# Block-sparse attention, cosine router and experts on one core: routing steps tied behind their unit in the queues of VectorE and ScalarE

## The chip, the core and the metric

One core of a Trainium2 chip: TensorE (matmuls), VectorE, ScalarE, GpSimd and the SP queue, which issues most transfers. The names in the profile are PE, PEld (TensorE's weight loads), DVE (VectorE), ACT (ScalarE), POOL (GpSimd) and SP. Each engine works through its own queue in the order in which it was written at build time; where an instruction waits, everything behind it on that engine waits too. The metric is the device time of one execution in microseconds (us); lower is better.

## What is computed

Block-sparse attention on q, k, v of 4 sequences, 8 heads, 768 tokens, 64 columns, and on its output, 3072 rows of 512, a router that sends each row to the best of 8 experts:

```python
scores = (1 / sqrt(64)) * q @ k.T
scores = where(mask, scores, -1e9)        # window, first and last block, 3 random blocks of 32
attn   = softmax(scores) @ v              # (4, 8, 768, 64)
x      = attn.transpose(0, 2, 1, 3).reshape(3072, 512)

xn     = x / (norm(x) + 1e-6)
logits = xn @ en.T / tau                  # en: 8 normalised expert vectors
expert = argmax(logits);  gate = softmax(logits)[expert]
out[rows of e] = gate * (relu(x @ w1[e]) @ w2[e])     # w1 512x1024, w2 1024x512
```

## The kernel before

**Attention.** Heads are taken in pairs; a pair has two halves of 384 queries, a half six blocks of 128 keys. One block of keys is a **unit**: 12 units a pair, 48 a sequence, 192 in all (`attention_fast`, L735). A unit's work: `score_fast` (L287) makes `sc` on TensorE, mask included, and ScalarE's exponential of it, `e` (L300); `attend_fast` (L304) adds `e` into `esum` on VectorE (L313 for the second block, L315 for the later ones; the first block has no sum) and multiplies `e` with v into `av` on TensorE (L318). Scores are made two units ahead. `av` has one PSUM buffer: after a half's last block ScalarE copies one part of it (`part`, L322) and VectorE adds the other to it, giving `at` (L324); only then may `av` of the next half begin. After the sixth block of each half `turn_fast` (L267) turns half of the next pair's keys and queries: matmuls into `turn`, then `kt` on VectorE (L283) and after it `qt` on ScalarE (L284).

**Settling a half.** Three units into the next half, `settle` (L328) turns `at` back on TensorE (`back`, L346 and L353; the router's products are computed along with it) and VectorE divides: `dens`, `inv`, `x`, `part` (L356 to L364). `squares` (L368) then sums the squares of x on GpSimd: one product and seven halving additions into `nsq`. `turn`, `back`, `rk`, `slot_ps` and the first expert tile's transposes share one PSUM buffer (`two_banks`).

**Routing.** When a sequence's 48 units are done, its rows are routed beside the next sequence's units. `route` (L418) is a generator in four steps: sums of squares (`nrm`, L427), GpSimd's power for the root (L428) and the logits' sum `l` (L436); normalising and the maximum (L438 to L443); the exponential `ex_l` on ScalarE (L446) and the choice of the expert, `oh` (L449 to L452); the gate (L455 to L457), x out to memory on the SP queue (L460), and on GpSimd the running counts `seen` (L464). `rank` (L468) counts rows by expert, three small matmuls `rk` and three VectorE steps. After sequence 1, `dispatch_early` (L561) gives the first two sequences' rows places in 5 expert tiles, in nine steps; `fetch` issues the first tiles' weights and rows, `prepare` turns the first tile's rows. The plan in `after_sequence` (L698) names the local unit (counted from 0 in each sequence) ahead of whose `attend_fast` each step is called.

**What sets the order.** The text's order is a proposal only: at build time a scheduler lists each engine's instructions by a model of when they become ready. It may put a step well ahead of the unit with which it is called.

**Experts.** 27 tiles of 128 rows, each 32 + 32 matmuls (`hp`, L676, two passes each), ReLU to `h` (L679 on ScalarE, L683 on VectorE), transposes of the next tile's rows, 8 matmuls `yp` (L689) and the gate's product (L691). Inside the first tile `last_rows` (L835) settles the last half, sums its squares and routes the last sequence; `between` (L826) ranks it and places the late rows.

Of the kernel before, what the change touches and what calls it, by code (L numbers as in the profile page):

```python
# [11 lines left out]
F32 = mybir.dt.float32  # L12
I32 = mybir.dt.int32
BF16 = mybir.dt.bfloat16
ACT = mybir.ActivationFunctionType
ALU = mybir.AluOpType
# [3 lines left out]
P = 128  # L20
B, H, S, D = 4, 8, 768, 64
# [265 lines left out]
def score_fast(k, u):  # L287

    nc = k.nc
    g, qh, kc = u // (2 * NC), u // NC % 2, u % NC  # L290
    kt, qt = [t.rearrange("p c r t -> p (c r t)") for t in k.turned[g]]
    ps = k.big.tile([P, 2, 512], F32, name="sc", tag="big")
    queries = slice(qh * HALF, (qh + 1) * HALF)
    quarters = [(h, r, slice(kc * P + D * r, kc * P + D * (r + 1))) for r in range(2) for h in range(2)]
    for rows, cols, first in ((k.kmask, k.qmask, True), (kt, qt, False)):
        for h, r, keys in quarters:
            nc.tensor.matmul(ps[D * r:D * (r + 1), h, 0:HALF], lhsT=rows[D * h:D * (h + 1), keys],  # L297
                             rhs=cols[D * h:D * (h + 1), queries], start=first, stop=not first)
    e = k.ep.tile([P, 2, HALF], F32, name="e", tag="e")
    nc.scalar.activation(e, ps[:, :, 0:HALF], ACT.Exp)  # L300
    k.es[u] = e


def attend_fast(k, u):  # L304
    nc = k.nc
    g, qh, kc = u // (2 * NC), u // NC % 2, u % NC
    e, v = k.es[u], k.loaded[g][2]
    if kc == 0:
        k.av = k.acc.tile([P, 2, 512], F32, name="av", tag="av")
        k.first = e  # L310
    elif kc == 1:
        k.esum = k.sp.tile([P, 2, HALF], F32, name="esum", tag="esum")
        nc.vector.tensor_tensor(out=k.esum, in0=k.first, in1=e, op=ALU.add)  # L313
    else:
        nc.vector.tensor_tensor(out=k.esum, in0=k.esum, in1=e, op=ALU.add)  # L315
    for r in range(2):
        for h in range(2):
            nc.tensor.matmul(k.av[D * h:D * (h + 1), r, 0:HALF], lhsT=v[D * r:D * (r + 1), h, kc, :],  # L318
                             rhs=e[D * r:D * (r + 1), h, :], start=(kc == 0), stop=(kc == NC - 1))
    if kc == NC - 1:  # L320
        part = k.sp.tile([P, HALF], F32, name="part", tag="part")
        nc.scalar.copy(out=part, in_=k.av[:, 1, 0:HALF])  # L322
        at = k.sp.tile([P, HALF], F32, name="at", tag="at")
        nc.vector.tensor_tensor(out=at, in0=k.av[:, 0, 0:HALF], in1=part, op=ALU.add)  # L324
        k.done[u // NC] = (at, k.esum)
# [42 lines left out]
def squares(k, w):  # L368

    nc = k.nc  # L370
    b, j, qh = w // (2 * NPAIR), w // 2 % NPAIR, w % 2
    chunks = slice(qh * NQ, (qh + 1) * NQ)
    x = k.x[b][:, chunks, j * P:(j + 1) * P]
    sq = k.sp.tile([P, NQ, P], F32, name="sq", tag="sq", bufs=1)
    nc.gpsimd.tensor_tensor(out=sq, in0=x, in1=x, op=ALU.mult)  # L375
    width = P // 2
    while width:
        out = sq[:, :, 0:width] if width > 1 else k.nsq[b][:, chunks, j:j + 1]
        nc.gpsimd.tensor_tensor(out=out, in0=sq[:, :, 0:width], in1=sq[:, :, width:2 * width], op=ALU.add)  # L379
        width //= 2  # L380


def count_good(k):
# [314 lines left out]
def after_sequence(n, b):  # L698

    routing = partial(next, route(n, b), None)  # L700
    plan = [(7, routing), (9, routing), (10, routing), (12, routing), (13, partial(rank, n, b))]
    if b == EARLY - 1:
        step = partial(next, dispatch_early(n), None)
        plan += [(u, step) for u in (15, 16, 18, 20, 21, 22, 23, 24, 25)]
        plan += [(27, partial(fetch, n, 0)), (28, partial(fetch, n, 1)), (43, partial(prepare, n, 0))]
    return plan


def attention_fast(n, ctx):
# [25 lines left out]
    for u in range(units):  # L735
        g = u // per
        if u % per == 0 and g + 2 < pairs:
            load_pair(n, g + 2)
        if u % NC == 3 and NC < u < units - 2 * NC:
            settle(n, u // NC - 1)  # L740
        if u % NC == 4 and NC < u < units - 2 * NC:
            squares(n, u // NC - 1)
        if u % (per * NPAIR) == 0 and u:
            plan = after_sequence(n, u // (per * NPAIR) - 1)
        for when, what in plan:
            if when == u % (per * NPAIR):
                what()
        attend_fast(n, u)
        if u + 2 < units:
            score_fast(n, u + 2)  # L750
        if u % NC == NC - 1 and g + 1 < pairs:
            turn_fast(n, g + 1, u % per // NC)
        if u in (units - NC - 1, units - 2):
            settle(n, u // NC - 1)
        if u == units - 4:
            squares(n, 2 * B * NPAIR - 3)


def attention_exact(n, ctx):
# [53 lines left out]
def fast(n):  # L813
    n.rings = {}
    with ExitStack() as ctx:
# [18 lines left out]

        def last_rows():  # L835
            settle(n, 2 * B * NPAIR - 1)
            squares(n, 2 * B * NPAIR - 2)
            squares(n, 2 * B * NPAIR - 1)
            for _ in route(n, B - 1):
                pass  # L840

# [90 lines left out]
```

## Time and profile before

| | |
|---|---|
| median of 3 runs | 807.51 us (807.42 to 809.67) |
| the profiled execution | 808.88 us |
| its span, first to last instruction | 807.2 us |
| TensorE busy | 754.6 us, 93% |
| VectorE, ScalarE, GpSimd busy | 41%, 25%, 25% |
| granted TensorE clock, mean | 0.98 |

The profiled execution's time lies 1.7 us above its span, which is what goes on around the first and the last instruction. TensorE is busy nearly throughout: attention fills the span up to about 397 us, the expert tiles the rest. Shares over the whole span say little of single stages; the rows below cut out the stretches in which a finished sequence is routed, and a quiet stretch beside them.

### The profile page before, as it was taken

The numbers are of one execution on the slowest core, as the hardware profiler recorded it, in microseconds if no ns is written. First come the engines' busy times: TensorE is split into PE (matmuls) and PEld (weight loads), VectorE is DVE, ScalarE is ACT, GpSimd is POOL, SyncE is SP. The second block draws the span as 40 slices with busy tenths as digits, with TensorE's granted clock in tenths as the row PEclk, the third lists the DMA queues.
The fourth block names the chain that finished last, engine by engine and source line by source line (L and its number), as shares of the span: only waits on it lengthen the run. The fifth ranks groups of instructions, "written<-read, shape, count | busy, mean of one in ns | idle before, by whom it ended". The sixth has DMA issues, their size and how long they took to land.

```text
span 807.2 us, 22564 instructions
## 1 busy us (share of the span) xinstructions
PE 754.6 (93%) x10028; PEld 492.9 (61%) x10028; DVE 327.1 (41%) x645; ACT 200.3 (25%) x292; POOL 205.2 (25%) x362
## 2 busy tenths in 40 slices
PE   5999979999698996999999999999999999999992
PEld 2555545555355553555676777867768677686770
DVE  3666665667576665566564111111111111111110
ACT  2555534555344453455300000000000000000000
POOL 2133342443325534234431211112111121110210
PEclk9999998999899998999999999999999999999997
DMA  4112215111349303200379998998999989889890
GB/s 157 25 59 62 62 60 218 55 45 45 138 154 401 129 31 126 74 2 4 122 278 406 332 341 323 321 339 299 338 323 322 343 309 335 329 317 334 302 327 15
DMA packets 64100, 165.48 MB, mean 205 GB/s; under 512 B 2988, under 2 KB 15276, under 8 KB 63222
## 3 DMA queue, kind: packets, MB, share of 16 engines
q1 hardware_dynamic: 59238, 149.60, 52.2%
q0 software_dynamic: 4480, 13.91, 4.4%
q8 instruction: 82, 1.34, 0.7%
q10 hardware_dynamic: 272, 0.39, 0.2%
q14 instruction: 28, 0.23, 0.1%
HBM read 148.14 MB, written 16.54 MB: 204 GB/s over the span
## 4 chain that ended last, share of the span: by engine, by line
PE 81%; issue 5%; DVE 5%; POOL 2%; ACT 2%; DMA 1%; another core or an unknown queue 0%; SPq 0%; POOLq 0%; DVEq 0%; ACTq 0%
PE hp L676 21%; PE yp L689 20%; PE sc L297 17%; PE av L318 15%; PE turn L280 2%; PE back L353 2%; ACT e L300 1%; PE xg_ps L661 1%; DVE esum L315 1%; PE back L346 1%; POOL sq L379 1%; DMA out_dram<-y,slot_l 1%; POOL nrm L428 1%; DMA emb<-in_moe_expert_emb_dram 1%; DVE esum L313 1%
## 5 line engine op out<-in xcount | busy, mean ns | idle before, releaser
L676 PEld LDWEIGHTS hp<-xgt,w 128*128 128x128 f32 x1728 | 197.1, 192 | 13.6 <-issue 11.5
L676 PE MATMUL hp<-xgt,w 128*128 128x128 f32 x1728 | 198.1, 275 | 1.4 <-DVE at L324 1.4
L689 PE MATMUL yp<-w,h 128*128 128x512 f32 x432 | 190.1, 592 | 0.9 <-DVE h L683 0.9
L300 ACT ACTIVATE e<-sc 128x768 f32<-128x768 f32 x192 | 155.4, 810 | 128.5 <-PE sc L297 124.5
L318 PE MATMUL av<-e,vld 64*64 64x384 f32 x1536 | 166.3, 500 | 20.0 <-DVE at L324 18.9
L315 DVE TENSOR_TENSOR esum<-esum,e 128x768 f32<-128x768 f32 x128 | 133.2, 1041 | 76.1 <-ACT e L300 73.8
L297 PE MATMUL sc<-qt,kt 64*64 64x384 f32 x1536 | 161.8, 489 | 0.1
L689 PEld LDWEIGHTS yp<-w,h 128*128 128x128 f32 x432 | 79.9, 190 | 91.7 <-issue 89.9
L679 ACT ACTIVATE h<-hp 128x512 f32<-128x512 f32 x27 | 16.1, 598 | 359.8 <-PE hp L676 359.8
L379 POOL TENSOR_TENSOR sq<-sq 128x192 f32<-128x192 f32 (+2 forms) x192 | 96.4, 502 | 15.1
L318 PEld LDWEIGHTS av<-e,vld 64*64 64x64 f32 x1536 | 51.4, 135 | 73.3 <-ACT e L300 24.2
L692 POOL DMA_INDIRECT out_dram<-y,slot_l x22 | 22.1, 1005 | 267.7 <-DVE y L691 255.6
L297 PEld LDWEIGHTS sc<-qt,kt 64*64 64x64 f32 x1536 | 60.1, 136 | 41.5 <-issue 38.9
L683 DVE TENSOR_SCALAR h<-hp 128x512 f32<-128x512 f32 x27 | 18.7, 692 | 160.1 <-PE hp L676 159.8
L375 POOL TENSOR_TENSOR sq<-x 128x384 f32<-128x384 f32 x32 | 26.9, 840 | 222.2 <-DVE part L364 168.3
L691 DVE TENSOR_SCALAR y<-yp,xg 128x512 f32<-128x512 f32 x27 | 20.3, 751 | 152.7 <-PE yp L689 152.7
L297 PE MATMUL sc<-qmask,kmask 64*64 64x384 bf16 x768 | 68.0, 330 | 0.0
L297 PEld LDWEIGHTS <-kmask 64*64 64x64 bf16 x768 | 25.2, 109 | 34.2 <-issue 34.1
L313 DVE TENSOR_TENSOR esum<-e 128x768 f32<-128x768 f32 x32 | 30.9, 966 | 16.8 <-ACT e L300 16.8
L284 ACT ACTIVATE qt<-turn 128x384 f32<-128x384 f32 x32 | 15.7, 491 | 49.5 <-DVE kt L283 49.5
L645 POOL DMA_INDIRECT xg<-x_dram,slot_l x24 | 24.8, 1032 | 7.4 <-issue 7.4
L353 PE MATMUL back<-ones,esum 64*64 64x1 f32 x1536 | 26.5, 191 | 0.0
(157 smaller groups left out, 374.6 us busy)
## 6 DMA issues: line engine op xcount, KB each, us to landing
w<-in_moe_w_dram SPq DMA_DIRECT2D x58, 2048.0 KB, 10.6
x_dram<-x SPq DMA_DIRECT2D x4, 1539.0 KB
kld<-in_k_dram SPq DMA_DIRECT2D x16, 384.0 KB, 4.5
vld<-in_v_dram SPq DMA_DIRECT2D x16, 384.0 KB, 3.3
qld<-in_q_dram SPq DMA_DIRECT2D x15, 384.0 KB, 5.6
x_early<-x SPq DMA_DIRECT2D x2, 1539.0 KB
qld<-in_q_dram ACTq DMA_DIRECT2D x1, 384.0 KB
xg<-x_dram,slot_l POOLq DMA_INDIRECT x24, 7.6
```

The source lines that it names most:

```text
L297: nc.tensor.matmul(ps[D * r:D * (r + 1), h, 0:HALF], lhsT=rows[D * h:D * (h + 1), keys], rhs=cols[D * h:D * (h + 1), queries], start=first ...
L300: nc.scalar.activation(e, ps[:, :, 0:HALF], ACT.Exp)
L313: nc.vector.tensor_tensor(out=k.esum, in0=k.first, in1=e, op=ALU.add)
L315: nc.vector.tensor_tensor(out=k.esum, in0=k.esum, in1=e, op=ALU.add)
L318: nc.tensor.matmul(k.av[D * h:D * (h + 1), r, 0:HALF], lhsT=v[D * r:D * (r + 1), h, kc, :], rhs=e[D * r:D * (r + 1), h, :], start=(kc == 0 ...
L353: nc.tensor.matmul(sums[D * s:D * (s + 1), t, h, r:r + 1], lhsT=esum[D * r:D * (r + 1), h, cols], rhs=k.ones[D * r:D * (r + 1), 0:1], star ...
L375: nc.gpsimd.tensor_tensor(out=sq, in0=x, in1=x, op=ALU.mult)
L379: nc.gpsimd.tensor_tensor(out=out, in0=sq[:, :, 0:width], in1=sq[:, :, width:2 * width], op=ALU.add)
L645: nc.gpsimd.indirect_dma_start(out=x[:, :], out_offset=None, in_=(k.x_dram if late else k.x_early)[:, :], in_offset=bass.IndirectOffsetOnA ...
L676: nc.tensor.matmul(hp[:, f, :], lhsT=w1[:, d, (f0 + f) * P:(f0 + f + 1) * P], rhs=xt[:, d, :], start=(d == 0), stop=(d == ND - 1))
L689: nc.tensor.matmul(yp, lhsT=h[:, f, :], rhs=w2[:, f, :], start=(f == 0), stop=(f == NF - 1))
L692: nc.gpsimd.indirect_dma_start(out=k.out[:, :], out_offset=bass.IndirectOffsetOnAxis(ap=slot, axis=0), in_=y[:, :], in_offset=None, bounds ...
```

## The change

Three edits. First, `score_fast` and `attend_fast` keep the last exponential and the last `esum` that they wrote, and every step of the plan is now called inside two blocks that tie each VectorE instruction of the step behind that `esum`, and each ScalarE instruction behind that exponential, in the engine's queue. It is an order only, no wait is added; instructions on other engines are not tied. Second, the plan calls nearly every step one unit later. Third, the squares of the last half go from GpSimd to ScalarE, one activation with an accumulator for each of three chunks, and the squares of the half before are called two units before the end of attention instead of in `last_rows`.

```diff
@@ score_fast
-    nc.scalar.activation(e, ps[:, :, 0:HALF], ACT.Exp)
+    k.exps = nc.scalar.activation(e, ps[:, :, 0:HALF], ACT.Exp)
@@ attend_fast (the same for the second block's sum, L313)
-        nc.vector.tensor_tensor(out=k.esum, in0=k.esum, in1=e, op=ALU.add)
+        k.summed = nc.vector.tensor_tensor(out=k.esum, in0=k.esum, in1=e, op=ALU.add)
@@ new
+def last_squares(k, w):
+    b, j, qh = w // (2 * NPAIR), w // 2 % NPAIR, w % 2
+    for c in range(qh * NQ, (qh + 1) * NQ):
+        sq = k.sp.tile([P, P], F32, name="sq_l", tag="sq_l")
+        k.nc.scalar.activation(sq, k.x[b][:, c, j * P:(j + 1) * P], ACT.Square,
+                               accum_out=k.nsq[b][:, c, j:j + 1])
@@ after_sequence
-    plan = [(7, routing), (9, routing), (10, routing), (12, routing), (13, partial(rank, n, b))]
+    plan = [(8, routing), (10, routing), (11, routing), (13, routing), (14, partial(rank, n, b))]
-        plan += [(u, step) for u in (15, 16, 18, 20, 21, 22, 23, 24, 25)]
-        plan += [(27, partial(fetch, n, 0)), (28, partial(fetch, n, 1)), (43, partial(prepare, n, 0))]
+        plan += [(u, step) for u in (16, 17, 18, 20, 21, 22, 23, 24, 26)]
+        plan += [(28, partial(fetch, n, 0)), (29, partial(fetch, n, 1)), (44, partial(prepare, n, 0))]
@@ attention_fast
-                what()
+                with n.tc.issue_after(n.summed.ins), n.tc.issue_after(n.exps.ins):
+                    what()
-        if u == units - 4:
-            squares(n, 2 * B * NPAIR - 3)
+        if u >= units - 4 and u % 2 == 0:
+            squares(n, 2 * B * NPAIR - 3 + (u == units - 2))
@@ last_rows
-            squares(n, 2 * B * NPAIR - 2)
-            squares(n, 2 * B * NPAIR - 1)
+            last_squares(n, 2 * B * NPAIR - 1)
```

What the scheduler makes of it, at three places. Line numbers of the changed kernel from L392 on are 9 higher than before (`nrm<-nsq` is L427 before and L436 after, `l<-part` L436 and L445).

VectorE, where sequence 0 is routed, before: from the end of the `settle` that gives the sequence's last x.

```order
L364 TENSOR_TENSOR part<-back,inv 128x3x16
L436 TENSOR_REDUCE l<-part 128x48
L427 TENSOR_REDUCE nrm<-nsq 128x6
L438 TENSOR_SCALAR nrm<-nrm 128x6
L439 RECIPROCAL nrm<-nrm 128x6
L441 TENSOR_TENSOR l<-l,nrm 128x48
L442 TENSOR_REDUCE mx<-l 128x6
L315 TENSOR_TENSOR esum<-esum,e 128x768
L443 TENSOR_TENSOR l<-l,mx 128x48
L449 TENSOR_SCALAR pick<-l 128x48
L450 TENSOR_TENSOR pick<-pick,rev 128x48
```

The same place after.

```order
L364 TENSOR_TENSOR part<-back,inv 128x3x16
L315 TENSOR_TENSOR esum<-esum,e 128x768
L324 TENSOR_TENSOR at<-av,part 128x384
L313 TENSOR_TENSOR esum<-e 128x768
L436 TENSOR_REDUCE nrm<-nsq 128x6
L283 COPY kt<-turn 128x2x3x64
L445 TENSOR_REDUCE l<-part 128x48
L315 TENSOR_TENSOR esum<-esum,e 128x768 x2
L447 TENSOR_SCALAR nrm<-nrm 128x6
L448 RECIPROCAL nrm<-nrm 128x6
L450 TENSOR_TENSOR l<-l,nrm 128x48
L451 TENSOR_REDUCE mx<-l 128x6
```

Before, `nrm<-nsq` and what needs it stand directly behind `part` and ahead of the half's last `esum` and of `at`; after, those two, the next half's first `esum` (L313) and more come first.

VectorE, where the early dispatch ends, before (`ge`, `val` and `lanes` are its tables of places).

```order
L585 SCALAR_TENSOR_TENSOR pos<-late,pos 128x12
L523 TENSOR_TENSOR ge<-pos,by_g 128x72
L526 TENSOR_REDUCE hi<-ge 128x12
L528 SCALAR_TENSOR_TENSOR low<-hi,pos 128x12
L529 TENSOR_TENSOR ge<-ge 128x12x5
L541 TENSOR_TENSOR lanes<-lane,low 128x384
L532 TENSOR_TENSOR val<-ge,tok_f 128x12x5 x2
L541 TENSOR_TENSOR lanes<-lane,low 128x384 x2
L315 TENSOR_TENSOR esum<-esum,e 128x768
L356 TENSOR_REDUCE dens<-back 128x6
L541 TENSOR_TENSOR lanes<-lane,low 128x384
L357 TENSOR_SCALAR dens<-dens 128x6
```

The same stage after: from `taken`, the rows that each expert takes, on.

```order
L587 SCALAR_TENSOR_TENSOR taken<-end_3772,base 128x8
L513 CAST expert_e<-ex 128x5
L315 TENSOR_TENSOR esum<-esum,e 128x768
L521 TENSOR_TENSOR at_e<-oh,base 128x96
L524 TENSOR_REDUCE pos<-at_e 128x12
L521 TENSOR_TENSOR at_e<-oh,taken 128x96
L593 TENSOR_TENSOR pos<-pos,rank 128x12
L524 TENSOR_REDUCE taken_t<-at_e 128x12
L592 TENSOR_TENSOR late<-rank,taken_t 128x12
L594 SCALAR_TENSOR_TENSOR pos<-late,pos 128x12
L324 TENSOR_TENSOR at<-av,part 128x384
```

Before, the tables of places stand ahead of the half's last sum and `at`; after, only the steps up to `pos` do, `ge` and all that follow it come behind L313.

ScalarE, from the last `part` of attention into the first expert tiles, before.

```order
L300 ACTIVATE e<-sc 128x768 x5
L322 COPY part<-av 128x384
L679 ACTIVATE h_6300<-hp_0_6301 128x512
L446 ACTIVATE ex_l<-l 128x48
L679 ACTIVATE h_6531<-hp_1_6532 128x512
```

After.

```order
L300 ACTIVATE e<-sc 128x768 x5
L322 COPY part<-av 128x384
L688 ACTIVATE h_6309<-hp_0_6310 128x512
L388 ACTIVATE sq_l,nsq<-x 128x128 x3
L455 ACTIVATE ex_l<-l 128x48
L688 ACTIVATE h_6528<-hp_1_6529 128x512
```

The three squares stand between the first tile's ReLU and the routing's exponential.

## Rows read from the trace of the kernel before

**Rows 1.** Busy time by stretch: length, five engines' busy time (instructions), PEclk, DMA, GB/s

```profile
110.95:130.37 19.42, 13.26 (x248) 7.00 (x242) 9.75 (x28) 5.76 (x9) 6.29 (x15) 0.82 0.40 164
130.37:142.61 12.24, 11.47 (x254) 6.70 (x246) 7.62 (x16) 5.62 (x8) 4.26 (x8) 1.00 0.34 99
142.61:153.34 10.73, 10.72 (x248) 6.11 (x242) 7.30 (x13) 5.62 (x8) 4.21 (x8) 1.00 0.01 3
226.19:251.55 25.36, 22.43 (x494) 12.90 (x486) 19.92 (x61) 11.24 (x16) 8.81 (x16) 1.00 0.63 221
251.55:276.09 24.54, 23.49 (x500) 13.75 (x493) 15.08 (x29) 11.24 (x16) 13.96 (x20) 1.00 0.68 259
309.63:328.69 19.06, 12.91 (x248) 6.89 (x243) 9.75 (x27) 5.76 (x9) 6.28 (x15) 0.82 0.21 84
```

**Rows 2.** Waits of TensorE, whole span: waiting, released by, total us, times, longest

```profile
PE av L318 <- DVE at L324: 18.9, 4, 6.2
PE rk L474 <- ACT qt L284: 2.3, 3, 0.8
PE turn L280 <- DVE part L364: 1.8, 1, 1.8
PE yp L689 <- DVE h L683: 0.9, 1, 0.9
PE first L661 <- ACT qt L284: 0.8, 1, 0.8
PE slot_ps L551 <- ACT qt L284: 0.7, 1, 0.7
```

**Rows 3.** Timeline of VectorE in the first route: start, us, instruction, idle before

```profile
115.89 0.18 DVE L427 TENSOR_REDUCE nrm<-nsq 128x6 f32<-128x24 f32 x1 [2.68 <-POOL nsq L379]
117.54 0.17 DVE L438 TENSOR_SCALAR nrm<-nrm 128x6 f32<-128x6 f32 x1 [1.47 <-POOL nrm L428]
118.33 0.95 DVE L315 TENSOR_TENSOR esum<-esum,e 128x768 f32<-128x768 f32 x1
120.78 0.56 DVE L324 TENSOR_TENSOR at<-av,part 128x384 f32<-128x384 f32 x1 [0.33 <-ACT part L322]
```

**Rows 4.** Timeline of VectorE in an undisturbed stretch

```profile
152.47 0.96 DVE L315 TENSOR_TENSOR esum<-esum,e 128x768 f32<-128x768 f32 x1 [0.65 <-ACT e L300]
156.75 0.56 DVE L324 TENSOR_TENSOR at<-av,part 128x384 f32<-128x384 f32 x1 [0.37 <-ACT part L322]
157.84 0.96 DVE L313 TENSOR_TENSOR esum<-e 128x768 f32<-128x768 f32 x1 [0.53 <-ACT e L300]
158.73 0.55 DVE L283 COPY kt<-turn 128x384 f32<-128x384 f32 x1
160.53 2.02 DVE L315 TENSOR_TENSOR esum<-esum,e 128x768 f32<-128x768 f32 x2 [1.26 <-ACT e L300]
```

**Rows 5.** Timeline of GpSimd: squares in the first route, then in the undisturbed stretch

```profile
113.25 2.33 POOL L379 TENSOR_TENSOR sq<-sq 128x192 f32<-128x192 f32 x6
...
155.65 3.51 POOL L379 TENSOR_TENSOR sq<-sq 128x192 f32<-128x192 f32 x6
159.24 0.20 POOL L379 TENSOR_TENSOR nsq<-sq 128x3 f32<-128x3 f32 x1
```

**Rows 6.** Timeline of TensorE in the undisturbed stretch

```profile
160.55 0.88 PE L318 MATMUL av<-e,vld 64*64 64x384 f32 x8
```

**Rows 7.** Timelines: ScalarE's only square, then GpSimd and VectorE in the first tile

```profile
7.78 0.63 ACT L166 ACTIVATE emb_sq<-emb 8x512 f32<-8x512 f32 x1 [5.24 <-DMA emb<-in_moe_expert_emb_dram]
8.32 0.19 ACT L166 ACTIVATION_READ_ACCUMULATOR emb_sq<-emb 8x1 f32 x1
...
403.57 0.83 POOL L375 TENSOR_TENSOR sq<-x 128x384 f32<-128x384 f32 x1 [3.49 <-DVE part L364]
...
407.22 0.18 DVE L427 TENSOR_REDUCE nrm<-nsq 128x6 f32<-128x24 f32 x1 [2.10 <-POOL nsq L379]
409.92 0.69 DVE L683 TENSOR_SCALAR h<-hp 128x512 f32<-128x512 f32 x1 [0.20 <-issue]
```

More of the change, by code (lines that the diff above doesn't have):

```diff
@@ L312, in attend_fast @@
         k.esum = k.sp.tile([P, 2, HALF], F32, name="esum", tag="esum")
-        nc.vector.tensor_tensor(out=k.esum, in0=k.first, in1=e, op=ALU.add)
+        k.summed = nc.vector.tensor_tensor(out=k.esum, in0=k.first, in1=e, op=ALU.add)
     else:
-        nc.vector.tensor_tensor(out=k.esum, in0=k.esum, in1=e, op=ALU.add)
+        k.summed = nc.vector.tensor_tensor(out=k.esum, in0=k.esum, in1=e, op=ALU.add)
     for r in range(2):
```

## Prediction

> **What bounds the kernel now.** I read the table of busy time by stretch first, cut at the starts of the `dens` step (L356), which comes once per half pair of heads. An undisturbed half pair lasts 10.73 us, and TensorE is busy for 10.72 of it, as in the stretch 142.61:153.34 [rows 1]: the attention half of the program runs at TensorE's pace, and whatever makes TensorE wait there lengthens the program one for one. From the first expert tile on, the list of waits names for TensorE only the 0.9 us at L689 [rows 2]; the rest is its own matmuls. So all that can be gained lies in waits of TensorE, and the same table shows where: the half pair in which a finished sequence is routed takes 19.42 us the first time and 19.06 the last; there are three such, after sequences 0, 1 and 2, and I take 19.2 for the middle one. Against 10.73 they lose 8.69, 8.5 and 8.33, together **25.5 us**. The half pair after each, with the ranking, takes 12.24: 1.51 too much.
>
> The list of waits says for what: `av` matmuls (L318) wait for VectorE's `at` (L324), 18.9 us in four waits, 6.2 the longest [rows 2]. VectorE's own timeline shows why `at` was late [rows 3]. In its queue `nrm` (L427) stood ahead of the running unit's `esum`; it waited 2.68 us for GpSimd's squares, then L438 waited 1.47 us for GpSimd's power, and only then came `esum`, the rest of the routing and `at`, at 120.78. [...]
>
> **The change part by part.**
>
> *Routing on VectorE (first edit and plan).* The order shows that the steps now stand where the text puts them: `nrm<-nsq` behind the `esum` of local unit 7, the next five steps behind that of unit 9, the one-hot steps inside the next `dens` chain, the gate's three ahead of `at`. So both waits for GpSimd leave the place ahead of `esum` and `at`. What is late next? I lay the new order over the undisturbed stretch.
> - First wait. There the squares' last add ended at 159.24 + 0.20 = 159.44 [rows 5] and `esum` L313 at 157.84 + 0.96 = 158.80 [rows 4]. So `nrm` still waits 0.64 us, runs 0.18, and `kt` (L283), due at 158.73, starts 0.9 us late. Queued behind `kt` are `qt` and the next exponential on ScalarE, and `av` on TensorE waits for that one: `esum` at 160.53 waited for it and `av` at 160.55 started with it [rows 4, 6], so there is no slack. I charge **0.9 us** of TensorE per route; bounds 0 (squares in time) and 2.7 (the wait of now [rows 3]).
> - What TensorE does not pay: the 0.9 us reduction `l<-part` falls into the gap of 1.26 before `esum` at 160.53 [rows 4]; the power, 1.5 us after `nrm`, runs beside two `esum`s of 2.02 us together, so L438 no longer waits.
> - Five short steps then stand before the next `esum`. Four took 117.54 to 118.33, 0.79 us [rows 3], five 1.0, against a gap of 0.65 [rows 4]: 0.35 late. Four more inside the `dens` chain fill its gaps, some 0.15; the gate's three, 0.55, stand against a gap of 0.37 before `at` [rows 4]. With 0.3 us given back at the `esum` between and TensorE a little behind `at`, **0.4 us** per route; bounds 0 and 0.9.
> - The clock: the waits that are left are of the size of the 1.8 us that TensorE waited at `turn` [rows 2], and the stretch with that one was granted 1.00, 226.19:251.55 [rows 1]. I charge nothing.
>
> So a route costs 1.3 instead of 8.5: 25.5 − 3 × 1.3 = **21.6 us** saved.
>
> What slows the squares shows in one row each: the six adds took 2.33 us while VectorE stood, and 3.51 beside its `esum`s [rows 5]. [...]
>
> *Ranking, one unit later.* TensorE's `rk` waited for `qt`, 2.3 us in three [rows 2], because it needs the PSUM buffer that `qt` was still reading. A unit later `qt` is over. Now GpSimd decides: its six `seen` adds stand alternating with the next squares, so the counts come about as late as TensorE does (their durations beside `esum`s are in no row). I charge 0.2 (0 to 0.8, the wait of now) instead of 0.77; the matmuls' own 0.75 (11.47 − 10.72 [rows 1]) stay. Saved: 3 × 0.57 = **1.7 us**. `count`, `mine` and `rank` now stand behind one more `esum`, ahead of which nothing on TensorE waits for them until `back`, a unit later.
>
> *Early dispatch (after sequence 1).* The two half pairs that hold ranking and dispatch take 25.36, 3.90 over 21.46; without the ranking's 1.51 the dispatch costs 2.4, seen as TensorE's 1.8 at `turn` and 0.4 at `at` [rows 1, 2]. VectorE was busy 19.92 instead of 14.60 there, so some 5.3 us of its work are the cause, and none of it goes away. By the place of the steps in the new order I estimate that 3.5 us of that stand ahead of `at` of unit 17 and 2.9 behind it, with the pauses between short dependent steps. The gaps there are 0.65, 0.3 and 0.37; with an estimated 0.5 that VectorE is ahead after `rk`, that leaves 1.7 late, and the rest against the next half pair's gaps 0.4. **2.1 instead of 2.4: 0.3 saved**; bounds 0 and 3.5 for the cost. `slot_ps` and the first tile's transposes move behind `qt` too: their waits of 0.7 and 0.8 [rows 2] go, **1.5 saved**. The rest of the stretch 251.55:276.09, some 2 us too long beside 8 MB of weights, stays as it is; the weights' and the rows' issues on the SP queue move by a unit and are needed only after the end of attention.
>
> On the SP queue the copies of `x` now stand between a pair's `vld` and `kld`, so `kld` waits for the gate's end, under 1 us later than now; the pair is turned one and a half pairs, some 30 us, later. Nothing.
>
> *Last squares on ScalarE.* Now GpSimd starts them at 403.57, `nrm` waits 2.10 us and runs at 407.22, L438 follows after the power, and `h` (L683) stands behind it at 409.92; TensorE waits 0.9 for `h` [rows 2, 7]. The order has three squares with an accumulator read each. The only such pair in the trace took 0.63 + 0.19 on 512 columns [rows 7], so at most 0.82 each on 128 columns, 2.5 us from 403.5: `nrm` runs before 406.1, at least 1.1 us earlier, and so does `h`, less 0.2 for L443 that now stands ahead of it. That covers the 0.9: **0.9 saved**, and as ScalarE's next work, the exponential, waits for the same chain, no cost. The squares of the half pair before only change their place in the text; GpSimd waits for their data as now.
>
> **The sum.** 21.6 + 1.7 + 0.3 + 1.5 + 0.9 = **26.0 us**. Against the profiled execution's own 808.88 us that gives 782.9. That execution lies 1.4 above the median of the runs, 807.51, so I predict **781.5**.
>
> **The rivals.**
> - *All hidden.* The waits that I charge (3 × 1.5 and 2.1, 6.6 us) vanish, as squares come in time and gaps take all steps: 774.9. For it speaks that several are under 1 us; against it that `av` at 160.55 has no slack.
> - *The wait moves and stays long.* `nrm` ahead of `kt` waits as it does now ahead of `esum`: 2.7 and the power's 1.5 come to stand before `kt`, the clock falls again for 2.3: 6.5 instead of 1.3 per route, 797.1. It decides if GpSimd ends its squares over 2 us later than in the undisturbed stretch. Against it: the overlay has them beside the same `esum`s already.
> - *No effect.* The order names a wait that was not the limit, and TensorE stands as long for another: 807.5. Against it, all three routes show the same rows.
> - *Slower: ScalarE is shut.* `ex_l` now stands behind the exponential of unit 12 and ahead of `part`, some 3 us after L443 should be through. Should L443 come more than 3 us late, exponentials and `part` queue behind `ex_l`, TensorE stands and its clock falls; from 12 us late on (3 + the 8.5 of now) each route is dearer than today. At 15 us, 3 × (12 + 2.5) = 43.5 against 25.5: 825. Nothing in rows 3 to 5 makes so long a chain.
>
> **How the numbers follow.** Forecast 0.75, all hidden 0.11, wait moved 0.09, no effect 0.02, slower 0.03. The forecast's own bounds: every charge at its lower end 774.9; step one at 2.7, the gate at 0.9, ranking at 0.8, dispatch at 3.5 make 5.4 + 1.5 + 1.8 + 1.4 = 10.1 more, 791.6. Both ends at once everywhere are unlikely; **776 to 789** leaves out about 2 in 10. A change under 0.3% (2.4 us) could not be told from none: faster 0.94, same 0.03, slower 0.03.
>
> **What would show it.** Right: no wait of `av` for `at` above 2 us after sequences 0 and 2; half pairs with routing of 11.5 to 12.5 us at a granted clock of 1.00; `nrm<-nsq` waiting under 1 us; `rk` not waiting for `qt`; `yp` not for `h`. Wrong: a stretch at half clock after a route, a long idle before `kt`, `ex_l` or `rk`, or `turn` waiting for a dispatch step for over 2 us.

## The result and the profile after

The changed kernel takes **781.9 us** (median of 4 executions, 780.66 to 785.54) against 807.46 for the kernel before in the same runs: ratio 0.9683 (95% interval 0.9652 to 0.9714), **25.6 us faster**. I had predicted 781.5, as 26.0 us. Two later sets of executions, on two chips, gave 780.51 at a ratio of 0.9672 (0.9659 to 0.9684) and 780.95 at 0.9668 (0.9651 to 0.9686).

The profiled execution of the first set took 785.54 (span 783.6), 3.6 us more than its median. Where it can't be read alone I set the profile of the second set beside it (span 779.9).

Busy time by stretch, changed kernel, cut at `dens` as [rows 1]: length, busy time of PE, PEld, DVE, ACT and POOL (with instructions), granted clock, DMA share, GB/s. First the three half pairs from the first route on, an undisturbed one, the first half pair of the second and third route, then the four half pairs of ranking, dispatch and weights after sequence 1 (49.90 us in the two stretches of [rows 1]), and the half pair with the last `at`:

```profile
111.56:123.41 11.85, 11.01 (x252) 6.21 (x246) 9.09 (x20) 5.51 (x8) 5.49 (x9) 1.00 0.01 2
123.41:135.11 11.70, 11.35 (x250) 6.82 (x246) 8.91 (x23) 5.74 (x9) 5.08 (x14) 1.00 0.65 198
135.11:146.88 11.77, 11.05 (x248) 7.05 (x243) 7.29 (x13) 5.61 (x8) 3.54 (x8) 1.00 0.44 176
146.88:157.62 10.74, 10.73 (x248) 6.13 (x243) 7.38 (x14) 5.61 (x8) 4.13 (x8) 1.00 0.37 113
200.54:212.40 11.86, 11.01 (x252) 6.23 (x247) 9.10 (x21) 5.51 (x8) 5.47 (x9) 1.00 0.01 3
295.00:306.85 11.85, 11.01 (x252) 6.22 (x246) 9.10 (x20) 5.51 (x8) 5.49 (x9) 1.00 0.01 3
212.40:262.30 49.90, 46.04 (x982) 29.08 (x978) 36.83 (x96) 22.70 (x33) 21.70 (x42) 1.00 0.87 302
372.79:381.39 8.60, 7.17 (x113) 6.58 (x106) 1.66 (x7) 1.07 (x2) 3.28 (x10) 0.80 0.83 283
```

The stretch with a route took 19.42 us at a clock of 0.82 and takes 11.85 at 1.00; all three show the same. In the trace of before the clock is 0.50 from 120.0 to 126.5 us, around the end of the 6.16 us that `av` waited for `at`. Two things are new: the third stretch, which took 10.73 before, takes 11.77, and the four half pairs of dispatch are as long as they were, though their waits for `qt` are gone. The list of TensorE's waits (us in total, times, longest) says what stands there now:

```profile
PE av L318 <- ACT e L300: 4.4, 5, 1.7
PE sc L297 <- issue: 2.3, 3, 1.1
PE hp L685 <- DVE at L324: 1.4, 1, 1.4
PE av L318 <- DVE at L324: 1.0, 3, 0.4
```

The 18.9 us that `av` waited for `at` [rows 2] have become 1.0; the waits at `rk`, `turn`, `yp`, `first` and `slot_ps` are no longer in the list. "issue" is a stop for which the profile has no releaser.

What remains of a route stands in the timeline of the first one, GpSimd, VectorE and TensorE (start, us, instruction, idle before it), to be read against [rows 3]:

```profile
113.86 3.50 POOL L379 TENSOR_TENSOR sq<-sq 128x192 f32<-128x192 f32 x6
117.67 0.18 DVE L436 TENSOR_REDUCE nrm<-nsq 128x6 f32<-128x24 f32 x1 [0.66 <-POOL nsq L379]
117.77 0.55 DVE L283 COPY kt<-turn 128x384 f32<-128x384 f32 x1
119.59 0.88 PE L318 MATMUL av<-e,vld 64*64 64x384 f32 x8 [0.84 <-ACT e L300]
...
127.18 0.52 DVE L324 TENSOR_TENSOR at<-av,part 128x384 f32<-128x384 f32 x1
127.75 0.88 PE L318 MATMUL av<-e,vld 64*64 64x384 f32 x8 [0.35 <-DVE at L324]
```

`nrm` still waits for GpSimd, 0.66 us now, with `kt` behind it, and `av` pays 0.84 for that; the gate ahead of `at` costs 0.35. Each value comes again in the other two routes.

In the tail the squares now take ScalarE 0.9 us, and `nrm` no longer waits:

```profile
382.69 0.31 ACT L388 ACTIVATE sq_l<-x 128x128 f32<-128x128 f32 x1 [1.91 <-DVE x L361]
382.91 0.19 ACT L388 ACTIVATION_READ_ACCUMULATOR sq_l<-x 128x1 f32 x1
383.49 0.19 ACT L388 ACTIVATION_READ_ACCUMULATOR sq_l<-x 128x1 f32 x1
383.89 0.17 DVE L436 TENSOR_REDUCE nrm<-nsq 128x6 f32<-128x24 f32 x1
386.82 0.69 DVE L692 TENSOR_SCALAR h<-hp 128x512 f32<-128x512 f32 x1 [0.20 <-DMA w<-in_moe_w_dram]
```

### The profile page after: what moved, and what is told of

It reads as the page before. It is cut to its first block, busy times and chain, and to the rows that moved or that the text cites. A ratio compares the mean times of both kernels' runs of the same rounds, so it can differ in the third digit from the quotient of the medians.

```text
span 783.6 us, 22560 instructions
## 1 busy us (share of the span) xinstructions
PE 751.3 (96%) x10028; PEld 496.4 (63%) x10028; DVE 329.5 (42%) x645; ACT 201.1 (26%) x298; POOL 199.2 (25%) x354
## 3 DMA queue, kind: packets, MB, share of 16 engines
q8 instruction: 82, 1.34, 0.7%
## 4 chain that ended last, share of the span: by engine, by line
PE 82%; issue 6%; DVE 6%; POOL 2%; DMA 2%; ACT 1%; SPq 0%; POOLq 0%; DVEq 0%; ACTq 0%
PE hp L685 22%; PE yp L698 21%; PE sc L297 17%; PE av L318 14%; PE turn L280 3%; DVE esum L315 2%; PE back L353 2%; PE xg_ps L670 1%; POOL sq L379 1%; PE back L346 1%; ACT e L300 1%; DMA out_dram<-y,slot_l 1%; DMA emb<-in_moe_expert_emb_dram 1%; DVE x L361 1%; PE qr L132 0%
## 5 line engine op out<-in xcount | busy, mean ns | idle before, releaser
L698 PE MATMUL yp<-w,h 128*128 128x512 f32 x432 | 189.9, 593 | 0.0
L318 PE MATMUL av<-e,vld 64*64 64x384 f32 x1536 | 162.4, 490 | 5.6 <-ACT e L300 4.4
L297 PE MATMUL sc<-qt,kt 64*64 64x384 f32 x1536 | 162.9, 486 | 1.7 <-issue 1.6
L315 DVE TENSOR_TENSOR esum<-esum,e 128x768 f32<-128x768 f32 x128 | 134.9, 1054 | 66.8 <-ACT e L300 64.2
L698 PEld LDWEIGHTS yp<-w,h 128*128 128x128 f32 x432 | 80.1, 190 | 90.3 <-issue 90.3
L379 POOL TENSOR_TENSOR sq<-sq 128x192 f32<-128x192 f32 (+1 forms) x186 | 91.4, 491 | 13.2
L318 PEld LDWEIGHTS av<-e,vld 64*64 64x64 f32 x1536 | 51.6, 133 | 57.1 <-ACT e L300 30.4
L692 DVE TENSOR_SCALAR h<-hp 128x512 f32<-128x512 f32 x27 | 18.7, 692 | 160.1 <-PE hp L685 159.8
L297 PEld LDWEIGHTS sc<-qt,kt 64*64 64x64 f32 x1536 | 60.3, 134 | 40.3 <-issue 37.7
L297 PE MATMUL sc<-qmask,kmask 64*64 64x384 bf16 x768 | 68.1, 325 | 0.7 <-issue 0.7
L297 PEld LDWEIGHTS <-kmask 64*64 64x64 bf16 x768 | 25.6, 108 | 32.8 <-issue 31.9
L313 DVE TENSOR_TENSOR esum<-e 128x768 f32<-128x768 f32 x32 | 31.0, 970 | 20.4 <-ACT e L300 20.4
```

The source lines that it names most:

```text
L313: k.summed = nc.vector.tensor_tensor(out=k.esum, in0=k.first, in1=e, op=ALU.add)
L315: k.summed = nc.vector.tensor_tensor(out=k.esum, in0=k.esum, in1=e, op=ALU.add)
L698: nc.tensor.matmul(yp, lhsT=h[:, f, :], rhs=w2[:, f, :], start=(f == 0), stop=(f == NF - 1))
```

## The experiments

Times are medians. Ratios are to the kernel before in the same set of runs, since chips differ: it took 806.75, 809.48 and 807.62 us in the three sets. The changed kernel itself ran in the first and the third set only; the kernels of the second (`dve_tie`, `pool_squares`, `x_dram_late`, `three_moves`) are set against its 0.9672 of the first. Their four profiles share a wait of `av` for `e` of 0.92 to 0.95 us at 248 to 254 us that no other profile has and whose cause is open, so 0.1% between sets says nothing.

### Which edit does it: the later unit or the ties?

Two kernels, each with one half of the change. `late_no_tie` leaves out the two blocks:

```diff
-                with n.tc.issue_after(n.summed.ins), n.tc.issue_after(n.exps.ins):
-                    what()
+                what()
```

> The changed kernel with every step one unit later, but without the ties; the last squares stay on ScalarE. The scheduler then puts VectorE's instructions of a route in the same order as in the kernel before, all of them ahead of at. Theory: the three stalls of 6.2 us with the slower clock behind them are back, and only the tail (0.9 us) is won: 805 to 807 us. Rival, the later unit finds the squares done and does the work: 782 to 786.

`tie_no_late` keeps the blocks and takes back the numbers of the plan:

```diff
-    plan = [(8, routing), (10, routing), (11, routing), (13, routing), (14, partial(rank, n, b))]
+    plan = [(7, routing), (9, routing), (10, routing), (12, routing), (13, partial(rank, n, b))]
```

(and so for the steps of the dispatch).

> The changed kernel with the ties, but every step at its old unit (7, 9, 10, 12, 13; 15 and so on). VectorE then has nrm<-nsq ahead of at again, with nothing of the later steps of the route ahead of it. Theory that both halves are needed: nrm waits for GpSimd until about 116.5 (its adds run at 2.3 us while VectorE stands still), l and at follow 0.2 and 0.84 us later, and the attention matmul starts 2.6 us late in each route, and the clock falls once more; 3 to 6 us per route against 1.1 now: 788 to 797 us. Rival, the ties alone do it: 782. Rival, the later unit alone does it: 806.

Measured: `late_no_tie` 805.55 us, ratio 0.9982 (0.9972 to 0.9992); `tie_no_late` 792.19, ratio 0.9811 (0.9797 to 0.9826). The stretch of the first route by engines, and VectorE's timeline in it, first of `late_no_tie`:

```profile
111.09:129.99 18.90, 12.76 (x248) 6.78 (x241) 9.74 (x27) 5.75 (x9) 6.27 (x15) 0.82 0.41 168
```

```profile
116.01 0.18 DVE L436 TENSOR_REDUCE nrm<-nsq 128x6 f32<-128x24 f32 x1 [2.66 <-POOL nsq L379]
117.66 0.17 DVE L447 TENSOR_SCALAR nrm<-nrm 128x6 f32<-128x6 f32 x1 [1.47 <-POOL nrm L437]
```

then of `tie_no_late`, the timeline with GpSimd's adds and TensorE:

```profile
111.83:127.33 15.50, 12.82 (x252) 6.94 (x246) 9.53 (x25) 5.72 (x8) 5.61 (x10) 0.89 0.01 3
```

```profile
114.13 2.91 POOL L379 TENSOR_TENSOR sq<-sq 128x192 f32<-128x192 f32 x6
117.35 0.18 DVE L436 TENSOR_REDUCE nrm<-nsq 128x6 f32<-128x24 f32 x1 [2.48 <-POOL nsq L379]
118.79 1.52 PE L318 MATMUL av<-e,vld 64*64 64x384 f32 x8 [2.68 <-DVE at L324]
```

The later unit alone does nothing to the routes: the scheduler lists VectorE's steps where it listed them before, and `nrm` waits 2.66 and L447 1.47, as in [rows 3]. The ties alone end the second wait but leave `nrm` ahead of `at`: 2.68 us of waiting, and a clock of 0.89. With both, the stretch goes 18.90, 15.50, 11.85. So the ties are what moves the work, and the unit decides behind which `esum` it comes to stand. The waits for `qt` go with the unit: TensorE's list in `late_no_tie` has none at `rk`, `slot_ps` or `first`, while `tie_no_late` still has

```profile
PE rk L483 <- ACT qt L284: 2.1, 3, 0.7
PE first L670 <- ACT qt L284: 0.8, 1, 0.8
PE slot_ps L560 <- ACT qt L284: 0.7, 1, 0.7
```

`late_no_tie` pays for it with one wait of 3.8 us for `at` in the dispatch, at 244.6 us.

### Is the tie on ScalarE needed?

`dve_tie` drops the second block only:

```diff
-                with n.tc.issue_after(n.summed.ins), n.tc.issue_after(n.exps.ins):
+                with n.tc.issue_after(n.summed.ins):
```

> The changed kernel with the tie behind esum (VectorE) alone and none behind e (ScalarE). VectorE's order stays word for word; on ScalarE ex_l<-l now stands three e ahead of its place. Theory: ScalarE waits at ex_l until l is there (written at 122.6 us in the first route), the e behind it (121.4 now) are 1.3 to 1.5 us late, and TensorE waits for them once in each route: 784 to 787 us, so the second tie is needed. Rival: the score matmuls run far enough ahead and nothing moves, 780.5 to 782.

Measured 783.28, ratio 0.9686 (0.966 to 0.9712), 0.15% above the changed kernel's 0.9672 and inside the intervals. Both theories are half right. ScalarE does stand at `ex_l`, as its row shows:

```profile
121.67 0.24 ACT L455 ACTIVATE ex_l<-l 128x48 f32<-128x48 f32 x1 [2.42 <-DVE l L452]
121.82 0.79 ACT L300 ACTIVATE e<-sc 128x768 f32<-128x768 f32 x1
```

but the next `e` comes at 121.82 and TensorE does not wait for it. The loss is in `av` behind `at`, 0.75 us in place of 0.35. My 784 to 787 counted ScalarE's delay as TensorE's.

### Is the rest of a route what the prediction charged it to?

`nrm_after_kt` ties the first step behind `kt` instead of `esum`:

```diff
-    nc.vector.tensor_copy(out=kt, in_=ps[:, :, 0])
+    k.ktc = nc.vector.tensor_copy(out=kt, in_=ps[:, :, 0])
...
-                with n.tc.issue_after(n.summed.ins), n.tc.issue_after(n.exps.ins):
+                with n.tc.issue_after(n.ktc.ins if when == 8 else n.summed.ins), n.tc.issue_after(n.exps.ins):
```

> The changed kernel, but the first step of a route is tied behind the copy kt instead of behind esum, so that the reduction nrm<-nsq, which waited 0.66 us for GpSimd, stands behind kt in VectorE's queue and not ahead of it. Theory: each of the three routes loses its 0.84 us wait of the attention matmul for e, 2.5 us in all, so 779.4 against 781.9, and the half pair with the first step takes 10.9 to 11.1 instead of 11.85 us. Rival: ScalarE's two copies (qt, then two e in a row) are late for another reason and the wait stays, 781.9.

Measured 777.83 against 780.51 for the changed kernel in the same set; ratio 0.9639 (0.9627 to 0.9651), outside the other's interval. The stretch of the first route, and `kt` and `nrm` in it:

```profile
110.79:121.82 11.03, 11.02 (x252) 6.23 (x246) 9.12 (x21) 5.62 (x8) 5.50 (x9) 1.00 0.01 2
```

```profile
116.18 0.54 DVE L283 COPY kt<-turn 128x384 f32<-128x384 f32 x1
116.92 0.18 DVE L436 TENSOR_REDUCE nrm<-nsq 128x6 f32<-128x24 f32 x1 [0.19 <-POOL nsq L379]
```

TensorE is busy for 11.02 of 11.03 us. The step was sized rightly: one instruction in the wrong place in the queue cost 0.83 us a route. `two_moves` adds that the gate's three instructions are tied behind `at` (`13: n.added`, where `n.added` is the instruction that writes `at`).

> nrm behind kt and the three instructions of gate behind at, the stores as in the changed kernel. Theory: 3 x 0.84 and 3 x 0.35 us of waits are gone, 3.5 us: 0.9955 of the changed kernel of this batch (777.0 where that is 780.5). Rival: the later store of x brings the late stop of TensorE further along and gives back up to 1 us, so it is no better than nrm_after_kt alone (0.9966).

Measured 778.56, ratio 0.9647 (0.9624 to 0.9669); the changed kernel, run once more beside it, took 780.95:

> The changed kernel, word for word, as the yardstick of this batch: 0.967 of the kernel before. If the short stops of TensorE that follow the stores (138 and 226 us) come from the order of the program, they are at the same places here, 0.4 to 1.7 us long.

In the trace of `two_moves` both waits are gone, and the half pair with the ranking takes 11.23 at 11.23 busy:

```profile
111.36:122.39 11.03, 11.01 (x252) 6.23 (x246) 9.12 (x21) 5.62 (x8) 5.50 (x9) 1.00 0.01 2
122.39:133.62 11.23, 11.23 (x250) 6.83 (x246) 8.55 (x24) 5.74 (x9) 5.08 (x14) 1.00 0.62 194
133.62:145.38 11.76, 11.06 (x248) 7.04 (x242) 7.29 (x14) 5.62 (x8) 3.53 (x8) 1.00 0.48 189
```

In the medians the gate's share is lost in the scatter: 2.4 us for both moves, less than the 2.7 of the one.

### The tail

`pool_squares` gives the last squares back to GpSimd:

```diff
-            last_squares(n, 2 * B * NPAIR - 1)
+            squares(n, 2 * B * NPAIR - 2)
+            squares(n, 2 * B * NPAIR - 1)
```

> The changed kernel with the squares of the last half pair back on GpSimd, and those of the half pair before it back in their old place. Theory: nrm waits 2.1 us for GpSimd in the tail, h is late for yp by 0.9 us: 0.9 us longer, 781.4 to 782.8, and a wait of yp for h of 0.9 us in the trace. Rival: TensorE's other work covers it and nothing changes. The first stretch of hp after the last at runs at either clock (3.84 or 5.47 us for 32 matmuls); that difference of 1.6 us is told apart in the trace.

Measured 787.04, ratio 0.9701 (0.9674 to 0.9728), 0.3% above the changed kernel's 0.9672, with overlapping intervals. The wait is back (`PE yp L698 <- DVE h L692: 0.9, 1, 0.9` in its list). But from the first `hp` after the last `at` to the end of the span it takes 786.6 − 374.8 = 411.8 us and the changed kernel 783.6 − 374.7 = 408.9, both with that `hp` at 5.47 us: 2.9 us, not 0.9. Of these, 1.2 are spent by the time of the ranking's matmuls (`rk` starts 18.76 us after that `hp` against 17.56): the wait, and 0.27 us more for two groups of matmuls in place of one. The other 1.7 lie behind the last instruction of any engine that the timeline shows. These are the last rows, first of `pool_squares` (span 786.6), then of the changed kernel (span 783.6):

```profile
772.22 0.99 POOL L701 DMA_INDIRECT out_dram<-y,slot_l  x1 [12.11 <-DVEq L815]
```

```profile
770.87 0.99 POOL L701 DMA_INDIRECT out_dram<-y,slot_l  x1 [12.11 <-DVEq L815]
```

The span ends 13.4 us after the end of the first and 11.7 after that of the second. The kernel before has 13.4 too, the profiles with the squares on ScalarE 11.2 to 12.0. What fills these microseconds no row names, so this part of the gain is measured and not explained.

### The stops that no data explain

`after_again` is the changed kernel once more:

> The changed kernel once more, word for word. Its first profile has three idle stretches of TensorE that no data explain: 0.72 us ahead of the score matmuls of L297 at 138.8, 1.68 us ahead of the attention matmul of L318 at 227.9 (the e it reads was written 2.2 us earlier) and 1.09 us ahead of L297 at 236.1; that execution took 785.54 us where the others took 780.7 to 781.9. Theory A: these stretches belong to that one execution, so a second profile lacks most of them and spans 779 to 781. Theory B: they come from the new order, so they stand at the same places with the same 3.5 us in all.

Measured 780.51. Its list has `PE sc L297 <- issue: 0.4, 1, 0.4` and `PE av L318 <- issue: 0.8, 1, 0.8`: the stops at 138 and 226 us are there again, at the same matmuls, but shorter; that at 236 is not. Theory B holds for the two places, A for the size. In `after_third` the stop at 138 us is 0.96 us and that at 226 us only 0.23, less than I had expected there. In the execution of `after_again` the four half pairs of the dispatch, and the first two of them alone, took

```profile
211.73:258.25 46.52, 45.05 (x982) 26.86 (x978) 36.78 (x95) 22.71 (x33) 21.68 (x42) 1.00 0.90 324
211.73:223.43 11.70, 11.35 (x250) 6.82 (x246) 9.93 (x31) 5.75 (x9) 5.08 (x14) 1.00 0.66 196
223.43:235.39 11.96, 10.97 (x248) 6.11 (x242) 11.20 (x37) 5.73 (x8) 3.62 (x8) 1.00 1.02 367
```

46.52 us, not 49.90. The stop at 138 us is in eight of the nine profiles of kernels that issue both stores of x among the loads of that pair: 0.4 to 1.5 us. The ninth is `tie_no_late`, which issues them some 3 us later and has no stop there; it has three, of 0.4 to 1.1 us, at 233, 242 and 248 us.

What it is, the queues show. From 124 to 136 us the changed kernel's transfers are these (queue, packets, MB, share of the 16 engines):

```profile
q1 hardware_dynamic: 824, 2.64, 70.4%
```

and nothing else. The instruction queue q8, which brings 0.02 MB every 5 to 6 us in undisturbed stretches, has no packet between those at 123.63 and 136.45 us, while x_early, x_dram, K, Q and V pass (4.2 MB in all, 2.64 of them by 136 us). What a packet of q8 holds no row tells. I take q8 for the queue of TensorE's instructions, with some 256 of them in a packet, as an estimate from three numbers of this trace: TensorE issues 248 + 243 matmuls and weight loads in the 10.74 us of an undisturbed half pair, so 256 in 5.6; from 38.10 to 111.50 us a packet came every 5.65 us on average, with gaps of 4.7 to 6.8; and in the whole span q8 has 82 packets (1.34 MB, 16.4 KB each) and TensorE 20,056 matmuls and weight loads, 245 a packet.

Two counts in the fourteen traces fit this. In them TensorE's stops of 0.4 us or more that the lists call "issue" are 18, and each ends 2.3 to 2.6 us after the start of a q8 packet; so do the eight waits at 224 to 228 us that the lists put to `e`. And if TensorE's records (matmuls, weight loads and its sequencer's) are counted in order of time, the number ahead of each of these 26 stops is 193 more than a multiple of 256: 5313 at 138 us, 9153 at 226. The waits for `kt` leave 184, 204 and 2 instead, those of `rk` for `qt` 113, 133 and 187. So the stops stand at one place in every 256 records, the waits do not, and after each stop TensorE goes on 2.3 to 2.6 us after a packet of q8 began. I read that as TensorE at the end of a block of instructions, waiting for the next.

Three kernels test what holds the packets back. `x_dram_late` issues only x_early there and x_dram 45 us later, behind the loads of another pair:

```diff
-    for dram in (k.x_early, k.x_dram):
-        if dram is k.x_dram or b < EARLY:
-            nc.sync.dma_start(out=dram[b * S:(b + 1) * S, :]...
+    store(k.x_early if b < EARLY else k.x_dram)
...
+    if b < EARLY:
+        store(k.x_dram)
+        yield
```

> The changed kernel, but of the two stores at the end of an early route only x_early stays there; x_dram (1.5 MB, read only by the late tiles) is issued some 45 us later, behind the loads of a later pair. In the changed kernel both stores stand among the loads of K, Q and V; from 123 to 136 us the trace has no packet in the instruction queue, whose packets otherwise come every 5 to 6 us, and at 138 us TensorE stops for 0.4 to 1.3 us with nothing to wait for. Theory: TensorE has run out of instructions, because their load stands behind 4.2 MB of data; with 1.5 MB less the stop is gone, the half pair after the first rank takes 10.8 instead of 11.5 to 12.4 us, and the stop of 0.85 to 1.7 us at 226 us shrinks too: 778.0 to 779.5 against 780.5 to 781.9. Rival: the stop has another cause, or the loads of K, Q and V are enough for it, and the time stays at 780.5 or above.

Measured 783.7, ratio 0.968 (0.9664 to 0.9696): no gain. Half pairs behind the first ranking, and those into which the two late stores now fall:

```profile
134.90:145.84 10.94, 10.94 (x248) 7.04 (x242) 7.28 (x13) 5.62 (x8) 4.14 (x8) 1.00 0.07 21
178.03:189.10 11.07, 11.07 (x248) 7.80 (x243) 7.37 (x14) 5.72 (x8) 4.14 (x8) 1.00 0.22 86
270.11:282.20 12.09, 11.56 (x252) 7.27 (x247) 7.97 (x15) 5.73 (x8) 4.14 (x8) 1.00 0.13 55
```

The stop at 138 us shrinks to some 0.2 us (10.94 against 10.73): q8's packet starts at 135.34, 12.0 us after the one before, and TensorE goes on at 137.71. The stop at 226 us does not shrink as I had expected; it is 0.86 us, and 0.85 in `after_again`. The late stores give back 0.3 us at 178 and 0.85 at 270 (12.09 against 11.24 in the changed kernel), 0.53 of the latter a stop of the same kind. And in `three_moves`, the same store moves on top of the two of `two_moves`, a stop of 0.57 us stays at 137 us: without x_dram, 2.7 MB are left in that piece, and the two kernels stop there for some 0.2 and for 0.57 us.

> Three moves on top of the changed kernel: nrm behind kt (as in nrm_after_kt), the three instructions of gate tied behind at instead of ahead of it, and x_dram stored later (as in x_dram_late). Theory: the costs add, 2.5 us of the first wait, 3 x 0.35 us of the wait for at, 1 to 2 us of the stops without a cause in the data: 775 to 776.5 us. Rival: seen comes 0.6 us later because x is stored later, rank's matmuls wait for it, and the gate's 0.35 us comes back there: 776 to 777.5. Rival: the later store collides with other loads and gives back its gain, 777.8.

It took 779.86, ratio 0.9632 (0.9614 to 0.9651), no better than `nrm_after_kt` alone at 0.9639. The time is that of the second rival, the cause is not: beside the late stores the half pairs take 10.73 and 11.24 us here, as in the changed kernel. The third move had little to give, as 0.57 us of the stop at 137 us and 1.33 of that at 224 us stay.

`stores_apart` takes the stores of the first route out of the middle of the loads, by calling the gate five units later there:

```diff
-    plan = [(8, routing), (10, routing), (11, routing), (13, routing), (14, partial(rank, n, b))]
+    plan = [(8, routing), (10, routing), (11, routing), (13, routing), (14, partial(rank, n, b)),
+            (18 if b == 0 else 13, routing)]
```

(the `seen` adds become a step of their own at unit 13; the rest as in `two_moves`).

> As two_moves, but in the first route alone gate and with it both stores (3 MB) come five units later, behind the loads of K, Q and V and not among them. Theory that TensorE runs out of instructions when 4.2 MB in one piece hold back the instruction queue: the packets of that queue come between the loads (126 to 130 us) and the stores (139 to 147), the stop at 138 us is gone and the half pair after the rank takes 10.8 instead of 11.5 to 12.4 us; 0.5 to 1 us less than two_moves. Rival, the stop sits at that place of the program for another reason: it stays at 137 to 138 us with 0.4 us or more.

Measured **777.38, ratio 0.9625 (0.9605 to 0.9644)**, the lowest of all, though its interval overlaps that of `two_moves`, so the trace has to decide. Its transfers from 124 to 138 us, and the half pair behind the ranking:

```profile
q1 hardware_dynamic: 816, 1.18, 29.2%
q8 instruction: 2, 0.03, 0.9%
```

```profile
134.06:144.79 10.73, 10.72 (x248) 6.11 (x242) 7.75 (x16) 5.62 (x8) 4.21 (x8) 1.00 0.53 221
```

Two instruction packets come between loads and stores, and the half pair is undisturbed: 10.73 against 11.76 in `two_moves`. The same 4.2 MB passed, in two pieces.

`more_store` does the opposite, a store more in the third route, which had no stop:

```diff
+    if b == EARLY:
+        nc.sync.dma_start(out=k.x_more[:, :].rearrange("(p c) w -> p (c w)", c=NC),
+                          in_=x.rearrange("p c w -> p (c w)"))
```

> The changed kernel with one store more: in the third route, which has only one store of 1.5 MB and no stop behind it, x is also stored into a third buffer that nobody reads, so that the traffic there is that of the first route. Theory (instructions held back by 4.2 MB): a stop of 0.4 to 1.3 us appears in the half pair behind the third rank, which now takes 10.73 us: 11.1 to 12 us. Rival: nothing happens there, 10.73 us.

It took 780.59, and the theory as I had put it failed:

```profile
316.18:326.91 10.73, 10.72 (x248) 6.11 (x242) 7.29 (x14) 5.62 (x8) 4.21 (x8) 1.00 0.48 190
```

No stop, with the traffic of the first route. Here one packet of q8 came at 311 us, amid the traffic, and one at 319; in the first route the last came at 123, before the traffic, and the next at 136. So the amount alone does not decide. Nor does the length of the gap alone: `dve_tie` stops after 11.7 us without a packet and `x_dram_late` hardly after 12.0, and in `tie_no_late` 8.6 us are too long at 242 us, where the packet before had come late as well. By the reading above, what counts is whether the next packet is there before TensorE reaches the end of its block; that is an estimate from the 26 stops, which all ended 2.3 to 2.6 us after a packet's start. Why one got through at 311 us, and none at 129 us in the first route, is open.

## Why the prediction was right, point by point

**Routes: right in mechanism and size.** Charged 1.3 us each, 0.9 at `kt` and 0.4 at `at`; measured 0.84 and 0.35, three times over, at a clock of 1.00. Route and ranking together cost 11.85 + 11.70 − 2 × 10.73 = 2.09 us in place of 19.42 + 12.24 − 21.46 = 10.20 [rows 1]; the prediction had 1.3 + 0.75 + 0.2 = 2.25. `nrm_after_kt` and `two_moves` show that both charges were what I took them for. That the squares are slower beside VectorE's sums shows again: the six adds took 3.50 us beside them, 2.91 in `tie_no_late`, where VectorE stood for part of the time. Why they are slower no row shows.

**The rival "the wait moves and stays long"** is nearly `tie_no_late`: `nrm` ahead of `at` waits 2.5 us, and the route costs 15.50 − 10.73 = 4.8. I had made it depend on GpSimd; it is the place in the queue that decides. The rivals set 2.3 and 2.5 us a route for the clock; in `tie_no_late` TensorE is busy for 12.82 us in the 15.50, at 0.89, and for 11.01 in the changed kernel's 11.85, at 1.00: 1.8.

**The ranking: right.** `rk` does not wait, neither for `qt` nor for the `seen` adds, which ended at 129.5 against `rk` at 130.8; the 0.2 us that I charged did not come. That it is the later unit that ends the wait for `qt` shows in `late_no_tie`.

**Early dispatch: the step that failed.** I gave the four half pairs 1.6 us (0.6 of the ranking, 0.3, and 0.7 at `slot_ps`); the first profile shows 49.90 as before, the second 46.52, which is 3.4. What ate the saving in the first is stops of TensorE of the kind above, at 193 more than a multiple of 256 records, which no term of mine had: 1.68 us ahead of `av` at 227.9 (by the list for `e`, which was 2 us old), 1.09 at 236.1 and 0.46 at 242.3, 3.2 in all against 0.85 in the second; the other 1.0 between the two is longer busy time of TensorE. Against that, two charges were too high. The dispatch's own VectorE work was to cost 2.1: in the second profile its half pair takes 11.96 with a stop of 0.85 in it, so about 0.4. And the "some 2 us" beside the weights, which I let stand, are 46.52 − 11.70 − 11.96 − 2 × 10.73 = 1.4 there.

**"Nothing" for the stores on the SP queue: wrong.** I asked only when `kld` is needed. The stores came 7 us later than before and the loads 7 us earlier, so that they fell together. In the 12.82 us from one packet of q8 to the next TensorE issued 521 matmuls and weight loads, and it stopped, by the reading above for want of instructions: 0.8 to 1.0 us in the half pair behind the first ranking in these two profiles, up to 1.8 in the others. In the kernel before, the stores were issued at 120.5 and the loads at 133.2, and TensorE stood for `at` for 6.16 us: the packets of q8 at 110.91 and 128.06 are 17.15 us apart, but it issued only 304 between them.

**The tail: mechanism right, mis-sized.** 0.9 predicted; 1.2 with the split group of matmuls, and 1.7 more behind the last instruction, which no term of mine had.

**What offset what.** In the median the errors cancel: routes and ranking came as predicted; the tail was 2.0 us better and the dispatch's two charges 2.3 too high; the stops, 1 to 4 us, and in some executions 1.6 of lower clock at the tail's `hp`, took that back. That the sum came within 0.4 us of the median is partly luck. In the first profile the gain was 23.6 us of span, with 3.9 us of stops, a start 0.6 us later, and the tail's `hp` at the lower clock.

## What to carry to other kernels

A scheduler's order is part of the kernel: with the last squares on ScalarE each time, calling the steps later gained 1.2 us here, tying them behind the work that they must not delay 14.6, and both together 26.2. Tie a step behind each instruction that somebody waits for (`kt`, `at`), not only behind the main loop's; the rest of the gain, 2.7 us, lay in one such place. When a step moves, move its transfers in mind as well: ask which loads they now fall among, and look in the DMA queues for the instruction queue's gaps. A stop without a cause can be tested by counting: here the number of TensorE's records ahead, 193 more than a multiple of 256 each time, told these stops from the waits for `kt` and `qt`.

## What the runs showed of the hardware

- **TensorE stopped while the instruction queue brought nothing.** With no packet in q8 for 11.7 to 13.5 us it stopped for 0.4 to 1.5 us at 138 us, with 193 records more than a multiple of 256 ahead (5313 in `after`); the profile calls such a stop "issue", or puts it to a producer that had ended 2.2 us before (`e`, ahead of `av` at 227.9). That TensorE had run out of instructions is my reading of these counts. With x_early, x_dram, K, Q and V in one piece (4.2 MB) the half pair behind the ranking took 11.76 us in `two_moves`, and with the same transfers in two pieces 10.73 in `stores_apart`; the same amount in the third route of `more_store` cost nothing, at 10.73.
- **After the same short idle the clock was lower in some executions and not in others.** TensorE waits 1.42 to 1.43 us for the last `at` in all fourteen profiles. In five of them the 32 `hp` matmuls after it take 5.47 us, in nine 3.84; the stretch above shows 0.80 for the first kind, 367.12:374.09 of `nrm_after_kt` 1.00 for the second. Both kinds occur with one and the same kernel (5.47 in `after_again`, 3.84 in `after_third`), so 1.6 us of a single profile can be this.
